# DeltaNet and a cosine router with experts: the last tile of each expert joined with the one before it, at widths sorted by size

## The chip, the cores and the metric

The kernel runs on one core of a Trainium2 chip. It is judged by the device time of one execution, in microseconds; several executions are taken and their median is given. TensorE (PE) multiplies matrices, VectorE (DVE) and ScalarE (ACT) work on rows of up to 128 partitions, GpSimd (POOL) issues the indirect transfers here, and SyncE (SP) issues the direct ones.

## The reference

Two blocks follow each other. The first is a delta-rule attention over 4 batches, 8 heads, 768 steps and 48 dimensions a head:

```python
k_n = k / (norm(k) + 1e-6)
for t in range(S):
    y[t] = q[t] @ state
    v_old = state.T @ k_n[t]
    state += beta[t] * outer(k_n[t], v[t] - v_old)
```

Its output, 3072 tokens of 384 numbers, goes through a router that sends each token to one of 8 experts (384 to 1024 to 384), all in float32:

```python
logits = normalized(x) @ normalized(expert_emb).T / tau
expert_idx = argmax(logits)
gate_w = softmax(logits)[expert_idx]
for e in range(8):
    mask = expert_idx == e
    out[mask] = gate_w[mask] * (relu(x[mask] @ w1[e]) @ w2[e])
```

On the given inputs the reference sends 385, 377, 351, 388, 365, 351, 421 and 434 tokens to experts 0 to 7.

## The kernel before, in words

**Attention and routing.** The 768 steps are cut into chunks of 64, and 24 units (12 chunks times two pairs of sequences, 128 tokens each) are worked through. A planner (`Plan`) holds every operation of this part with a cost and a due time and writes out one order for each engine. After each group of four units (two at the end) the router runs: TensorE counts for each token its place among those of its expert, and POOL writes the token's row number into a list in DRAM (`idmap`, one list of 3200 places for each expert, filled up with entries that point to an empty row and to no output). `run` holds where each list has got to. Token rows with their gate stand in DRAM too (`x_dram`).

When 16 of the 24 units are routed, `snap` notes how many tokens of expert 0 there are, at most 256 (`ahead`), and two early tiles of 128 of them are computed within the attention part, out of weights kept in `w1_first` and `w2_first`.

**Expert stage.** The rest begins when the last tokens are on the lists (line 1101 on). Here the order on each engine is the order of the code. The tiles are of 128 tokens of one expert. DVE works out on one partition how many tiles each expert has (`tiles`, at least one), a running sum over experts (`ends`, lines 1189 to 1191, seven additions one after another), and from it for every tile number the expert and the place of its list (`info`). SP reads these into registers (`where`, lines 1126 and 1127) and issues the read of the tile's list (`read_ids`); POOL gathers its rows by that list (`read_x`); SP loads the expert's two matrices, 1.5 MB each, into rings of three (`read_w1`, `read_w2`).

A tile then has three steps on TensorE: `transposed` turns its rows (three transposes, a copy by DVE), `hidden` makes 24 matmuls of 128 columns into two PSUM banks (a ReLU by ACT each), and `result` makes eight matmuls of 384 columns into one bank; DVE multiplies by the gate and POOL scatters the rows to the output. In `work_through` the order is: gather for tile i+3, hidden of i, first matrix of i+3, transposes of i+1, result of i, second matrix of i+3, list of i+5. The first tile takes its weights from `w1_first` and `w2_first`.

There are up to 31 tiles. The first 22 always run; four more run if there are more than 22 (line 1256), five more if there are more than 26 (line 1258). The branches read the number from a register that every engine has loaded (line 1227).

## Time and profile before

| | |
|---|---|
| median of 9 runs | 645.83 us (641.39 to 649.39) |
| profiled execution | 641.89 us, span 640.2 us |
| granted TensorE clock, mean over the span | 0.912 |
| TensorE busy | 546.0 us (85%) |
| DVE, ACT, POOL busy | 42%, 28%, 26% |
| expert stage | first transposes at 340.4 us, last result at 626.8 us, end 640.2 us |
| tiles in the expert stage | 26 |
| moved by DMA | 115.46 MB, of which 50 loads of 1.5 MB are experts' matrices |

The times of an operation are from one profiled execution. A record of TensorE is one pass; a float32 matmul shows as two records. Records overlap, so the distance from one start to the next tells what a record costs, and not its own length. "Idle before" is the time in which an engine stood still ahead of an operation, with what ended it.

### The profile page before, as it was taken

What the parts mean: (1) busy time and instruction counts of PE and PEld (TensorE: products, weight loads), DVE (VectorE), ACT (ScalarE), POOL (GpSimd) and SP (SyncE); (2) the same over time, 40 slices, a digit from 0 to 9 for tenths busy, and PEclk for the clock granted to TensorE, in tenths of its full rate; (3) what the DMA queues carried; (4) which work ended last, traced back from release to release, by engine and by line L of the source; (5) the groups of instructions that cost most, each with busy time, mean ns of one, the idle gap of its engine ahead of it and who ended that gap; (6) DMA issues with size and microseconds to landing.
All of it is one profiled execution on the core that took longest, in us unless ns stands there. A gap on an engine that the chain in (4) does not pass through costs nothing. (4 is left out here: it accounts for less than half of the span.)

```text
span 640.2 us, 22729 instructions
## 1 busy us (share of the span) xinstructions
PE 546.0 (85%) x9995; PEld 459.4 (72%) x9995; DVE 267.2 (42%) x749; ACT 180.1 (28%) x327; POOL 167.7 (26%) x217
## 2 busy tenths in 40 slices
PE   3573688688788888788997999999999999999991
PEld 3462678587677877677875787878787878787880
DVE  4898768669889877823141111010111111111100
ACT  2222535526637345464420010101111111111010
POOL 4434334154362221312121211212121212121100
PEclk9995788559989779989997999999999999999996
DMA  4444744533414311132015999999999899999500
GB/s 75 81 80 85 198 73 78 128 63 67 107 36 103 93 45 26 64 98 81 31 40 199 390 387 388 387 348 304 339 319 333 305 341 319 337 312 331 201 17 6
DMA packets 127911, 115.46 MB, mean 180 GB/s; under 512 B 83754, under 2 KB 113873, under 8 KB 127810
## 3 DMA queue, kind: packets, MB, share of 16 engines
q1 hardware_dynamic: 122242, 102.93, 52.0%
q0 software_dynamic: 4480, 10.85, 4.6%
q8 instruction: 80, 1.31, 0.8%
q10 hardware_dynamic: 1088, 0.20, 0.2%
q14 instruction: 21, 0.17, 0.1%
HBM read 102.02 MB, written 12.72 MB: 179 GB/s over the span
## 5 line engine op out<-in xcount | busy, mean ns | idle before, releaser
L1164 ACT ACTIVATE hT<-acc 128x512 f32<-128x512 f32 x52 | 31.1, 597 | 259.5 <-PE acc L1162 259.5
L1162 PEld LDWEIGHTS acc<-xTm,w 128*128 128x128 f32 x816 | 93.8, 192 | 4.5
L1162 PE MATMUL acc<-xTm,w 128*128 128x128 f32 x816 | 93.9, 275 | 0.0
L1169 PE MATMUL acc<-w,hT 128*128 128x384 f32 x272 | 90.5, 486 | 0.0
L1172 POOL DMA_INDIRECT out_dram<-y,ids x26 | 26.3, 1010 | 205.2 <-DVE y L1171 195.4
L1169 PEld LDWEIGHTS acc<-w,hT 128*128 128x128 f32 x272 | 50.4, 190 | 31.5
L1154 DVE COPY xTm<-acc 128x384 f32<-128x384 f32 x26 | 14.5, 558 | 134.6 <-PE acc L1153 134.6
L565 DVE TENSOR_TENSOR w_first<-w_first,tmp 128x30 f32<-128x30 f32 (+9 forms) x180 | 68.3, 381 | 3.9
L561 DVE TENSOR_TENSOR tmp<-w_first 128x30 f32<-128x30 f32 (+9 forms) x180 | 67.2, 375 | 4.1
L1171 DVE TENSOR_SCALAR y<-acc,xg 128x384 f32<-128x384 f32 x26 | 16.1, 618 | 125.0 <-PE acc L1169 125.0
L273 PE MATMUL psum_pair<-KQ 48*32 48x64 f32 (+2 forms) x2304 | 50.2, 280 | 15.2 <-DVE w_first L546 7.2
L273 PEld LDWEIGHTS psum_pair<-KQ 48*32 48x32 f32 (+1 forms) x2304 | 42.9, 142 | 20.6 <-issue 9.5
L1162 PEld LDWEIGHTS acc<-xTm,w_first 128*128 128x128 f32 x432 | 51.5, 198 | 3.3 <-DVE xTm L1154 1.2
L1162 PE MATMUL acc<-xTm,w_first 128*128 128x128 f32 x432 | 51.7, 281 | 0.8 <-DVE xTm L1154 0.8
L1169 PE MATMUL acc<-w_first,hT 128*128 128x384 f32 x144 | 47.9, 486 | 0.0
L273 PE MATMUL psum_pair<-S,KQ 48*64 48x64 f32 x1408 | 34.7, 243 | 9.4 <-issue 4.1
L1169 PEld LDWEIGHTS acc<-w_first,hT 128*128 128x128 f32 x144 | 26.7, 190 | 16.7
L273 PEld LDWEIGHTS psum_pair<-S,KQ 48*64 48x64 f32 x1408 | 29.8, 154 | 12.2 <-issue 5.3
L276 ACT ACTIVATE KQ<-psum_pair 128x1024 f32<-128x1024 f32 x24 | 24.6, 1024 | 44.8 <-PE psum_pair L309 35.3
L1137 POOL DMA_INDIRECT xg<-x_dram,ids x26 | 25.3, 972 | 38.5 <-DMA ids<-idmap 22.9
L960 POOL DMA_INDIRECT idmap<-tokid,slots_i x24 | 24.1, 1006 | 39.1 <-DVE slots_i L936 12.6
L615 POOL TENSOR_TENSOR V<-v,sqb 128x384 f32<-128x384 f32 x24 | 20.6, 864 | 50.3 <-DVE R L670 32.6
(183 smaller groups left out, 737.4 us busy)
## 6 DMA issues: line engine op xcount, KB each, us to landing
w<-in_moe_w_dram SPq DMA_DIRECT2D x34, 1536.0 KB
w_first<-in_moe_w_dram SPq DMA_DIRECT2D x16, 1536.0 KB
q<-in_q_dram SPq DMA_DIRECT2D x96, 48.0 KB
v<-in_v_dram SPq DMA_DIRECT2D x48, 96.0 KB
w_first<-in_k_dram SPq DMA_DIRECT2D x88, 48.0 KB
x_dram<-XC SPq DMA_DIRECT2D x5, 800.0 KB
idmap<-space SPq DMA_DIRECT2D x1, 2048.0 KB
w_first<-in_moe_w_dram SPq DMA_DIRECT2D x6, 256.0 KB
```

The source lines that it names most:

```text
L273: nc.tensor.matmul(out_, lhsT=lhsT, rhs=rhs, start=start, stop=True, skip_group_check=True)
L276: nc.scalar.activation(out_, in_, ACT.Copy, scale=scale)
L561: nc.vector.tensor_tensor(t, X[:, j + 1:, j:j + 1].broadcast_to([128, rows, j]), X[:, j:j + 1, 0:j].broadcast_to([128, rows, j]), op=ALU.mult)
L565: nc.vector.tensor_tensor(X[:, j + 1:, 0:j], X[:, j + 1:, 0:j], t, op=ALU.subtract)
L615: nc.gpsimd.tensor_tensor(buf("V", m)[:, i * 2 * NP * D:(i + 1) * 2 * NP * D].rearrange("p (jj j d) -> p jj j d", jj=2, d=D), buf("v", m)[ ...
L960: put = nc.gpsimd.indirect_dma_start(out=idmap[:, :], out_offset=bass.IndirectOffsetOnAxis(ap=slot_i[:, i:i + 1], axis=0), in_=K["tokid"][ ...
L1137: t.read = nc.gpsimd.indirect_dma_start(out=t.x, out_offset=None, in_=x_dram[:, :], in_offset=bass.IndirectOffsetOnAxis(ap=t.ids[:, 0:1], ...
L1162: nc.tensor.matmul(psH[:, i, :], lhsT=t.w1[:, j, (f + i) * 128:(f + i + 1) * 128], rhs=t.xT[:, j, :], start=(j == 0), stop=(j == KC - 1))
L1164: nc.scalar.activation(t.hT[:, f:f + 4, :], psH, ACT.Relu)
L1169: nc.tensor.matmul(psO, lhsT=t.hT[:, f, :], rhs=t.w2[:, f, :], start=(f == 0), stop=(f == NF - 1))
L1171: nc.vector.tensor_scalar_mul(y, psO, t.x[:, Dm:Dm + 1])
L1172: nc.gpsimd.indirect_dma_start(out=out[:, :], out_offset=bass.IndirectOffsetOnAxis(ap=t.ids[:, 1:2], axis=0), in_=y, in_offset=None, bound ...
```

## The change

The two early tiles stay. After them:

- The tile that follows takes 160 tokens of expert 0 (`FIRST`). What is left of each expert's list is cut into whole tiles of 128 and one tail that is whatever remains after them, between 129 and 256 tokens for the larger experts, less for a short list, and zero or below where nothing is left. So the number of whole tiles is the number of 128s less two, at least zero.
- Tails are ranked by size on DVE and run from the largest to the smallest at fixed widths, 256, 256, 224, 224, 192, 192, 160 and none (`WIDTHS`). Where a tail doesn't fit its width (`misfit`), another arm of a branch runs eight tails of 256.
- In a tile of more than 128 tokens the hidden layer is made in matmuls as wide as the tile, two of them to a PSUM bank. The rows are gathered, transposed and scattered in blocks of up to 128.
- The result of a block of 128 is as before. One of 96, 64 or 32 rows is made in parts of 64 and 32: with 64 rows, matmuls go by turns to the two column halves of the array (PSUM partitions 0 to 63 and 64 to 127), with 32 to its four quarters, and the partial sums are added by ACT and DVE.
- The order: the first tile, five whole tiles, the tails, then the whole tiles that remain, in a branch for more than five and one for more than ten. Rings are made a class, so that both arms of the branch begin at the same buffer; the index buffers for items from the fourth on are 16 new ones, gathered rows have 10 buffers in place of 6, results 6 in place of 4.
- The running sum is one multiplication with a triangle of ones (`not_after`) and one reduction. 16 operations on DVE are added that work out and sort the tails, ten on POOL and one on DVE that set constants, and one in `snap`. Two numbers are loaded into registers on every engine in place of one.
- Item 3's rows are gathered twice: once ahead of `chain` and once by it, into the same buffer.

The core of the diff:

```diff
+FIRST = 160
+WIDTHS = (256, 256, 224, 224, 192, 192, 160, 0)
...
-    nth = cpool.tile([1, NT, 1], F32, name="nth")
+    nth = cpool.tile([1, WHOLE, 1], F32, name="nth")
...
         nc.gpsimd.memset(zrow, 0.0)
+        nc.gpsimd.memset(not_after, 1.0)
+        nc.gpsimd.affine_select(out=not_after, in_=not_after, compare_op=ALU.is_ge, fill=0.0, base=0,
+                                pattern=[[1, E], [-1, E]], channel_multiplier=0)
+        for i, w in enumerate(WIDTHS):
+            nc.gpsimd.memset(widths[:, i:i + 1], float(w))
 
...
     def snap():
         nc.vector.tensor_scalar_min(ahead, run[0:1, 0:1], float(AHEAD * T))
         nc.vector.tensor_copy(ahead_i, ahead)
+        nc.vector.tensor_scalar_add(base_e[:, 0:1], ahead, float(FIRST))
 
...
-    w1_ring = ring("w1_", 3, [128, KC, F], ex, first=[w1_first])
-    w2_ring = ring("w2_", 3, [128, NF, Dm], ex, first=[w2_first])
-    x_ring = ring("xg", 6, [128, ROW], ex)
-    xT_ring, hT_ring, y_ring = (ring(name, n, shape, ex) for name, n, shape in (
-        ("xTm", 2, [128, KC, T]), ("hT", 2, [128, NF, T]), ("y", 4, [128, Dm])))
-    banks = ring("acc", 8, [128, 512], pe)
+    class Ring:
+
+        def __init__(r, name, n, shape, pool, dtype=F32, first=()):
+            r.ts = list(first) + [pool.tile(shape, dtype, name=f"{name}{i}") for i in range(n - len(first))]
+            r.taken = 0
+            turning.append(r)
+
+        def __call__(r):
+            r.taken += 1
+            return r.ts[(r.taken - 1) % len(r.ts)]
+
+    turning = []
+    w1_ring = Ring("w1_", 3, [128, KC, F], ex, first=[w1_first])
+    w2_ring = Ring("w2_", 3, [128, NF, Dm], ex, first=[w2_first])
+    x_ring = Ring("xg", 10, [128, ROW], ex)
+    more_ids = Ring("more_ids", 16, [128, ID], ex, I32)
+    xT_ring, hT_ring, y_ring, part_ring = (Ring(name, n, shape, ex) for name, n, shape in (
+        ("xTm", 2, [128, KC, 2 * T]), ("hT", 2, [128, NF, 2 * T]), ("y", 6, [128, Dm]), ("part", 6, [128, Dm])))
+    banks = Ring("acc", 8, [128, 512], pe)
 
...
     class Tile:
-        pass
-
-    def where(t, i):
-
-        if i == 0:
+
+        def __init__(t, width, place):
+            t.width, t.place, t.ids, t.x = width, place, [], []
+
+    def sizes(t):
+        return [min(T, t.width - o) for o in range(0, t.width, T)]
+
+    def where(t):
+        kind, i = t.place
+        if kind == "first":
             t.e, t.s = 0, nc.values_load(ahead_i[0:1, 0:1], engines=(SP,), min_val=0, max_val=AHEAD * T)
         else:
-            t.e = nc.values_load(info[0:1, 0, i:i + 1], engines=(SP,), min_val=0, max_val=E - 1)
-            t.s = nc.values_load(info[0:1, 1, i:i + 1], engines=(SP,), min_val=0, max_val=NMAP - T)
-
-    def read_ids(t):
-        t.ids = ids_ring()
-        read = nc.sync.dma_start(t.ids, idmap[bass.ds(t.s, T), :])
-        for put in lists[-1]:
-            tc.add_manual_dep(read.ins, put.name, AFTER, reason="tokens' lists are complete")
+            table = info if kind == "whole" else ends_info
+            t.e = nc.values_load(table[0:1, 0, i:i + 1], engines=(SP,), min_val=0, max_val=E - 1)
+            t.s = nc.values_load(table[0:1, 1, i:i + 1], engines=(SP,), min_val=0, max_val=NMAP - 2 * T)
+
+    def read_ids(t, source):
+        where(t)
+        for b in range(len(sizes(t))):
+            t.ids.append(source())
+            read = nc.sync.dma_start(t.ids[b], idmap[bass.ds(t.s + b * T, T), :])
+            for put in lists[-1]:
+                tc.add_manual_dep(read.ins, put.name, AFTER, reason="tokens' lists are complete")
 
     def read_x(t):
-        t.x = x_ring()
-        t.read = nc.gpsimd.indirect_dma_start(
-            out=t.x, out_offset=None, in_=x_dram[:, :],
-            in_offset=bass.IndirectOffsetOnAxis(ap=t.ids[:, 0:1], axis=0))
+        for b in range(len(sizes(t))):
+            t.x.append(x_ring())
+            t.read = nc.gpsimd.indirect_dma_start(
+                out=t.x[b], out_offset=None, in_=x_dram[:, :],
+                in_offset=bass.IndirectOffsetOnAxis(ap=t.ids[b][:, 0:1], axis=0))
 
...
     def transposed(t):
         t.xT = xT_ring()
-        psX = acc([128, KC, 128])
-        for j in range(KC):
-            nc.tensor.transpose(psX[:, j, :], t.x[:, j * 128:(j + 1) * 128], ident)
-        nc.vector.tensor_copy(t.xT, psX)
+        for b, n in enumerate(sizes(t)):
+            psX = acc([128, KC, 128])
+            for j in range(KC):
+                nc.tensor.transpose(psX[:, j, 0:n], t.x[b][0:n, j * 128:(j + 1) * 128], ident[0:n, 0:n])
+            nc.vector.tensor_copy(t.xT[:, :, b * T:b * T + n], psX[:, :, 0:n])
 
     def hidden(t):
         t.hT = hT_ring()
-        for f in range(0, NF, 4):
-            psH = acc([128, 4, T])
-            for i in range(4):
+        k = 4 if t.width <= T else 2
+        for f in range(0, NF, k):
+            psH = acc([128, k, t.width])
+            for i in range(k):
                 for j in range(KC):
-                    nc.tensor.matmul(psH[:, i, :], lhsT=t.w1[:, j, (f + i) * 128:(f + i + 1) * 128], rhs=t.xT[:, j, :],
-                                     start=(j == 0), stop=(j == KC - 1))
-            nc.scalar.activation(t.hT[:, f:f + 4, :], psH, ACT.Relu)
+                    nc.tensor.matmul(psH[:, i, :], lhsT=t.w1[:, j, (f + i) * 128:(f + i + 1) * 128],
+                                     rhs=t.xT[:, j, 0:t.width], start=(j == 0), stop=(j == KC - 1))
+            nc.scalar.activation(t.hT[:, f:f + k, 0:t.width], psH, ACT.Relu)
+
+    def columns(n):
+        if n in (T, T // 2, T // 4):
+            return [(0, n)]
+        return [(0, T // 2), (T // 2, T // 4)]
 
     def result(t):
-        psO = acc([128, Dm])
-        for f in range(NF):
-            nc.tensor.matmul(psO, lhsT=t.hT[:, f, :], rhs=t.w2[:, f, :], start=(f == 0), stop=(f == NF - 1))
-        y = y_ring()
-        nc.vector.tensor_scalar_mul(y, psO, t.x[:, Dm:Dm + 1])
-        nc.gpsimd.indirect_dma_start(
-            out=out[:, :], out_offset=bass.IndirectOffsetOnAxis(ap=t.ids[:, 1:2], axis=0),
-            in_=y, in_offset=None, bounds_check=N - 1, oob_is_err=False)
-
+        for b, n in enumerate(sizes(t)):
+            y = y_ring()
+            for o, w in columns(n):
+                q = T // w
+                psO = acc([128, Dm])
+                for f in range(NF):
+                    c = f % q * w
+                    nc.tensor.matmul(psO[c:c + w, :], lhsT=t.hT[:, f, b * T + o:b * T + o + w], rhs=t.w2[:, f, :],
+                                     start=(f < q), stop=(f >= NF - q))
+                if q == 1:
+                    nc.vector.tensor_scalar_mul(y, psO, t.x[b][:, Dm:Dm + 1])
+                    continue
+                total = psO[o:o + w, :]
+                for i in range(q):
+                    if i * w != o:
+                        part = part_ring()[o:o + w, :]
+                        nc.scalar.copy(part, psO[i * w:i * w + w, :])
+                        nc.vector.tensor_tensor(y[o:o + w, :], total, part, op=ALU.add)
+                        total = y[o:o + w, :]
+                nc.vector.tensor_scalar_mul(total, total, t.x[b][o:o + w, Dm:Dm + 1])
+            nc.gpsimd.indirect_dma_start(
+                out=out[:, :], out_offset=bass.IndirectOffsetOnAxis(ap=t.ids[b][0:n, 1:2], axis=0),
+                in_=y[0:n, :], in_offset=None, bounds_check=N - 1, oob_is_err=False)
+
+    first = Tile(FIRST, ("first", 0))
+    read_ids(first, ids_ring)
+    first.w1, first.w2 = w1_ring(), w2_ring()
+    read_x(first)
 
     nc.vector.tensor_tensor(run, run, base_e, op=ALU.subtract)
-    nc.vector.tensor_tensor(run[:, 0:1], run[:, 0:1], ahead, op=ALU.subtract)
+    over = thr.rearrange("p e n -> p (e n)")
     nc.vector.tensor_tensor(thr, run.unsqueeze(2).broadcast_to([1, E, N // T]), thr, op=ALU.is_gt)
     tiles = cpool.tile([1, 1, E], F32, name="tiles")
     nc.vector.tensor_reduce(tiles[:, 0, :], thr, axis=AX.X, op=ALU.add)
-    nc.vector.tensor_scalar_max(tiles[:, :, 0], tiles[:, :, 0], 1.0)
+    nc.vector.tensor_scalar(tiles, tiles, -2.0, 0.0, op0=ALU.add, op1=ALU.max)
     ends = cpool.tile([1, 1, E], F32, name="ends")
-    nc.vector.tensor_copy(ends, tiles)
-    for e in range(1, E):
-        nc.vector.tensor_tensor(ends[:, :, e], ends[:, :, e], ends[:, :, e - 1], op=ALU.add)
-    te = [1, NT, E]
-    done = cpool.tile(te, F32, name="done")
-    nc.vector.tensor_tensor(done, ends.broadcast_to(te), nth.broadcast_to(te), op=ALU.is_le)
-    which = cpool.tile([1, NT], F32, name="which")
+    upto = over[:, 0:E * E].rearrange("p (a b) -> p a b", a=E)
+    nc.vector.tensor_tensor(upto, tiles.broadcast_to([1, E, E]), not_after, op=ALU.mult)
+    nc.vector.tensor_reduce(ends[:, 0, :], upto, axis=AX.X, op=ALU.add)
...
+    whole = [Tile(T, ("whole", i)) for i in range(WHOLE)]
+    read_ids(whole[0], ids_ring)
+    read_x(whole[0])
+    tc.add_manual_dep(read_w1(whole[0]).ins, whole[0].read.ins.name, AFTER, reason="first tokens, then weights")
+    read_w2(whole[0])
+    read_ids(whole[1], ids_ring)
+    read_x(whole[1])
+    read_w1(whole[1])
+    read_w2(whole[1])
+
+    vals = cpool.tile([1, 3, E], F32, name="vals")
+    nc.vector.tensor_copy(vals[:, 0], sixteenths)
+    nc.vector.scalar_tensor_tensor(out=vals[:, 1], in0=tiles[:, 0], scalar=float(T), in1=base_e, op0=ALU.mult, op1=ALU.add)
+    nc.vector.scalar_tensor_tensor(out=vals[:, 2], in0=tiles[:, 0], scalar=-float(T), in1=run, op0=ALU.mult, op1=ALU.add)
+    nc.vector.tensor_tensor(vals[:, 2], vals[:, 2], sixteenths, op=ALU.subtract)
+    nc.vector.tensor_tensor(upto, vals[:, 2:3].broadcast_to([1, E, E]),
+                            vals[:, 2].unsqueeze(2).broadcast_to([1, E, E]), op=ALU.is_gt)
...
+    ends_info = cpool.tile([1, 2, E], I32, name="ends_info")
+    nc.vector.tensor_copy(ends_info, sorted_[:, 0:2])
+    misfit = cpool.tile([1, 2], F32, name="misfit")
+    nc.vector.tensor_tensor(sorted_[:, 2], sorted_[:, 2], widths, op=ALU.is_gt)
+    nc.vector.tensor_reduce(misfit[:, 0:1], sorted_[:, 2], axis=AX.X, op=ALU.add)
+    nc.vector.tensor_copy(misfit[:, 1:2], ends[:, 0, E - 1:E])
+    flags = cpool.tile([1, 2], I32, name="flags")
+    nc.vector.tensor_copy(flags, misfit)
+
+    transposed(first)
+
+    def chain(items, start, stop):
+
+        for i in range(start, stop):
+            t = items[i]
+            if i + 3 < len(items):
+                read_x(items[i + 3])
+            hidden(t)
+            if i + 3 < len(items):
+                read_w1(items[i + 3])
+            if i + 1 < len(items):
+                transposed(items[i + 1])
+            result(t)
+            if i + 3 < len(items):
+                read_w2(items[i + 3])
+            if i + 5 < len(items):
+                read_ids(items[i + 5], more_ids)
+
+    ahead_of_tails = 5
+    tails = [Tile(2 * T, ("end", i)) for i in range(E)]
+    items = [first] + whole[:ahead_of_tails] + tails
+    for t in items[3:5]:
+        read_ids(t, more_ids)
+    read_x(items[3])
+    bad, count = (nc.values_load(flags[0:1, i:i + 1], min_val=0, max_val=most) for i, most in ((0, E), (1, WHOLE)))
+    chain(items, 0, 1 + ahead_of_tails)
+
+    def arm(ws):
+
+        was = [r.taken for r in turning]
+        own = [copy.copy(t) for t in items[1 + ahead_of_tails:]][:len(ws)]
+        rest = [copy.copy(t) for t in whole[ahead_of_tails:]]
+        for t in own + rest:
+            t.ids, t.x = list(t.ids), list(t.x)
+        for t, w in zip(own, ws):
+            t.width = w
+        line = own + rest[:ahead_of_tails]
+        chain(line, 0, len(own))
+        with tc.If(count > ahead_of_tails):
+            chain(line, len(own), len(line))
+            with tc.If(count > 2 * ahead_of_tails):
+                line = rest[ahead_of_tails:]
+                for t in line[:5]:
+                    read_ids(t, more_ids)
+                for t in line[:3]:
+                    read_x(t)
+                    read_w1(t)
+                    read_w2(t)
+                transposed(line[0])
+                chain(line, 0, len(line))
+        for r, n in zip(turning, was):
+            r.taken = n
+
+    with tc.If(bad == 0) as cmp:
+        arm([w for w in WIDTHS if w])
+    with cmp.Else():
+        arm([2 * T] * E)
```

## The prediction

> **What bounds the kernel now.** I read the page's slices first (the TensorE row stands at 9 from 300 us on), then the busy time by stretch, then what TensorE waited for, then its timeline. The stretch from the first full-clock tile to the last matmul:
>
> ```profile
> 366.00:627.00 261.00, 260.75 (x1608) 209.26 (x1606) 27.89 (x48) 28.67 (x48) 44.69 (x45) 1.00 0.88 308
> ```
>
> The columns are PE, weight load, DVE, ACT, POOL, granted clock, DMA share, GB/s. TensorE is busy for all but 0.25 us of 261 at a granted clock of 1.00; DVE, ACT and POOL stand at a tenth to a sixth. DMA is loaded (0.88), but it does not hold TensorE up. From 340 us to 627 us TensorE's waits are these:
>
> ```profile
> PE acc L1153 <- DMA xg<-x_dram,ids: 4.4, 2, 3.9
> PE acc L1162 <- DVE xTm L1154: 0.8, 1, 0.8
> ```
>
> 3.9 and 0.8 of that belong to the start; no wait for weights (the DMA of `w`) is among them. So in this stage time is columns streamed through TensorE, and one tile is read off its start times:
>
> ```profile
> 366.57 5.52 PE L1162 MATMUL acc<-xTm,w 128*128 128x128 f32 x48
> 371.93 0.49 PE L1153 MATMUL acc<-ident,xg 128*128 128x128 f32 x3
> 372.26 5.33 PE L1169 MATMUL acc<-w,hT 128*128 128x384 f32 x16
> 377.42 5.52 PE L1162 MATMUL acc<-xTm,w_first 128*128 128x128 f32 x48
> ```
>
> Start to start: hidden 5.36 (48 records, two to a float32 matmul: 111.7 ns each at 128 columns), transposes 0.33 (0.11 each), result 5.16 (16 records, 322.5 ns each at 384 columns). A tile is 10.85 us, and 26 of them are 282.1. The two durations give a line for other widths: 6.3 ns + 0.823 ns a column.
>
> **What the inputs make of the code.** The reference's choices on the given inputs count 385, 377, 351, 388, 365, 351, 421 and 434 tokens for the eight experts. Less the 256 of expert 0 done early, that is 2+3+3+4+3+3+4+4 = 26 tiles, as the trace has (26 of L1172). After: a first tile of 160; 10 whole tiles; tails of 249, 237, 223, 223, 178, 165, 132 (expert 0 has none left), which fit widths 256, 256, 224, 224, 192, 192, 160 and drop the eighth. Columns fall from 3328 to 2944, weight pairs loaded from 25 to 17; row blocks gathered and scattered stay 26.
>
> **TensorE's work after.** By the line, a record at 160, 192, 224, 256 columns is 138.1, 164.4, 190.7, 217.1 ns; 48 of them 6.63, 7.89, 9.16, 10.42. A full block's result is 5.16. A remainder of 64 columns puts two matmuls on two column halves, one of 32 puts four on quarters; at full overlap that is 2.58 and 1.29. Transposes are 0.33 a block, less for narrow ones. So:
> 256: 10.42 + 10.32 + 0.66 = 21.40, twice 42.80.
> 224: 9.16 + 5.16 + 2.58 + 1.29 + 0.59 = 18.78, twice 37.56.
> 192: 7.89 + 5.16 + 2.58 + 0.51 = 16.14, twice 32.28.
> 160: 6.63 + 5.16 + 1.29 + 0.43 = 13.51, and the first tile the same.
> With 10 × 10.85 = 108.5 the sum is 248.2, which is **33.9 less** than 282.1.
>
> **The packing** is the price that the trace of before does not show: it never runs 128 rows on column groups. The nearest rows are the attention's, with rows and columns both split:
>
> ```profile
> 205.25 1.16 PE L273 MATMUL psum_pair<-S,KQ 48*64 48x64 f32 x64
> ...
> 175.25 2.15 PE L273 MATMUL psum_pair<-KQ 48*32 48x64 f32 x128
> ```
>
> The first: 64 records on four tiles in 1.16 us, about 15 ns each once the last one's 0.2 us latency is taken off, where one alone streams about 56 ns (half of 111.7): 3.7 of 4. The second has four column groups times two row halves, at half clock (a record alone is 112 ns): 16.8 ns each, over six of eight. So four column groups stream different data at once, but each over 48 rows. Ends: full overlap, no gain beyond it (the array has no more columns); or none, where all eight remainders cost 5.16, which is 4 × 2.58 + 4 × 3.87 = 25.8 more. I take 3.7 of 4, nearest to the first row: 7% of 15.5, or **+1.0**.
> The Trainium skill, "TensorE: Matmul & The Clock Gate", Part 3, "Measured speedup vs the span model", speaks against this: three column tiles of 32 gave 2.38, not 3. Taken for all remainders, my estimate from that page is +4.0 in place of +1.0, and the forecast would be 620.
>
> **Changing between array shapes.** Start to start, 128*128 transposes to 64*64 costs 0.20 us against 0.11 streaming, so 0.09 more; 48*64 of 96 columns (streaming 0.08) to 128*128 costs 0.25, so 0.17 more. The remainders make 14 changes (3 for each 224, 2 for each other); transposes of 64 and 32 rows up to 12 more. Ends 14 × 0.09 = 1.3 and 26 × 0.17 = 4.4; I take 20 × 0.13, **+2.6**.
>
> **Evictions.** A tail's hidden layer fills four banks of two slices; the ReLU of the last is needed by result matmul 6, some 3.9 us after the first, and an ACTIVATE takes 0.6. The partial sums add up to 4 ACT copies and 7 DVE operations a tile (0.56 to 0.62 for 384 columns), 2 and 4 us beside a step of 13 to 21 us on engines that are at 11%. Queued behind them is the next ReLU or xTm copy, whose reader comes 5 us later. 0; if that cover went, 4 us a tail.
>
> **The start.**
>
> ```profile
> 336.95 0.99 POOL L1137 DMA_INDIRECT xg<-x_dram,ids  x1 [4.88 <-PE psum_pair L1045]
> 338.25 1.01 POOL L1053 DMA_INDIRECT out_dram<-space,ids  x1 [0.31 <-issue]
> 339.56 0.99 POOL L1137 DMA_INDIRECT xg<-x_dram,ids  x1 [0.30 <-issue]
> 340.42 0.50 PEld L1153 LDWEIGHTS acc<-ident,xg 128*128 128x128 f32 x3 [4.48 <-issue]
> ```
>
> The first tile's second block is gathered in the slot of 338.25 (the early tile's store moves behind), lands 3.45 later as the first one did, at 341.7, is transposed and copied, and each engine now loads two flags (0.49 each on TensorE). Hidden starts at about 343.1 in place of 342.13: +1.0 (ends 0.2 and 1.9). POOL's queue gets a trap: item 3's tokens are gathered twice into the same buffer. The index rows of that tile are now issued behind two pairs of weights on SP's queue; one pair held an index row up from 346.1 to 354.8 before, so they land near 362, the first gather near 368 and the second near 374.4 (6.4 us to landing each), while TensorE wants them at 343.1 + 15.5 (tile one, at half clock to 346.2) + 10.85 + 5.36, about 374.8. Behind the second gather on POOL stand the stores of the first tile (nobody waits) and the next gather, wanted 11 us later. 0 to 3, taken 0.5. The old 0.7 wait at 361 goes. Sum **+0.8**.
>
> **What lies beside other work.** DVE's index chain ran from 329.02 to 335.17. Seven serial adds and wider compares go (some 2.4 us), two go in; then 16 operations for the tails, 0.13 to 0.41 each, 2.1 to 6.6. It ends between 336 and 340.5, before the flags are loaded at about 341.8; SP's first index load follows its own issue at 334.95 as before. The early tile's multiply, queued behind, is up to 4 us late and only its store waits. 0. Ten constants on POOL (0.09 to 0.42 each) fall before an idle time of 7.8 us at 20.7; one on DVE (0.15) before one of 1.0. 0. The add in the snapshot is 0.2 at most. SP issues 16 DMAs of weights fewer. Branches that fall through cost TensorE 0.09 (the one at 579.0), and the taken one cost 3.37 us but beside other work:
>
> ```profile
> L1258 PEldq COMPARE_BRANCH x2: 193/1781/3369, 622.3 to 626.9; - x2
> ```
>
> After the last matmul come another branch or two on POOL before the end (0.05 each as POOL's were, 3.4 as the PE's): **+0.5**.
>
> **Sum.** 33.9 - 1.0 - 2.6 - 0.8 - 0.5 = 29.0 less. The profiled execution took 641.9 us (span 640.2), so 612.9 on its scale. The median of the nine runs is 645.8, 3.9 above it; the attention part is left alone, so I subtract the same 29.0: **616.8**, say 617.
>
> **Rivals.**
> *Column groups overlap in part.* If four quarters run only two at a time (each float32 matmul is two records on one quarter, which may block the order), four remainders cost 2.58 in place of 1.29: +5.2, 622; half the overlap everywhere gives 630. For it: no row has 128-row column tiles. Against: 3.7 of 4 also with two records a matmul.
> *They don't overlap.* +25.8 less the 1.0 booked: 642, 0.6% faster.
> *Slower: the tails do not fit.* If the chip's counts put a sorted tail above its width (223 against 224 is the closest, twice), the other arm runs eight tails of 256: 171.2 + 108.5 + 13.5 = 293.2, 11.1 more than before; with 3.4 for the taken branch, 0.8 and 0.5 it is 662. It decides from two tokens routed differently from the reference. Against: tokens on the edge between two experts are few, and the trace's 26 tiles agree with the counts.
> *A new wait for tokens.* The doubled gather lands 5 us late: 622. For it: DMA share 1.04 from 355 to 367 us. Against: 17 weight pairs for 25, and tail steps of 13 to 21 us each need no more than one pair.
>
> **How the numbers follow.** Near-full overlap 0.68; partial overlap 0.15; none 0.07; wrong arm 0.05; new waits 0.05. The likeliest gives 617, by its own bounds 611 to 622. Partial overlap and new waits reach to 632; with them 0.88 is counted, the ends of each cut off, so 609 to 632 for 8 in 10. A measurement of this kernel tells about 0.5%, 3.2 us, from no change. Faster: all but the wrong arm and half of no overlap, 0.91; same 0.04; slower 0.05.
>
> **What would show it.** TensorE busy without a gap at clock 1.00 from 366 us to about 598; 256-wide hidden records near 217 ns; a 32-column remainder in 1.3 to 1.5 us and not 2.6 or 5.2; gaps of 0.1 to 0.2 where the shape changes; DMA share near 0.6; whole tiles still 10.85. It is wrong if remainders take over 3 us, if seven tails turn into eight of 256, or if TensorE waits for `xg` near 375.

## The result, and the profile after

The changed kernel takes 619.19 us (median of 20 runs, 615.21 to 623.23) where the kernel before took 646.36 beside it (62 runs). The ratio is 0.960, with a 95% interval of 0.958 to 0.962: 25.9 us less, 24.7 to 27.2. The forecast was 29.0 less. The profiled execution of the changed kernel took 617.59 us with a span of 615.7; that of the kernel before had 640.2.

The busy time by stretch, changed kernel, for the stretch that answers to 366 to 627 us before, and for the start of the experts' tiles (columns as there: PE, weight load, DVE, ACT, POOL, granted clock, DMA share, GB/s):

```profile
366.00:600.00 234.00, 234.00 (x1279) 179.24 (x1278) 33.02 (x63) 32.89 (x61) 47.08 (x48) 1.00 0.69 241
...
340.00:355.00 15.00, 9.61 (x45) 9.13 (x46) 1.34 (x3) 1.05 (x3) 3.94 (x4) 0.66 0.65 225
```

TensorE is still the bound: busy for all of 234 us at clock 1.00, with 1279 records where the longer stretch before had 1608. DVE and ACT have risen only from 27.9 and 28.7 to 33.0 and 32.9 us, so the added copies and sums are far from a limit, and the DMA share fell from 0.88 to 0.69. The second row is the one place in the expert stage, up to its last matmul, where the clock is down; it is taken up below.

What TensorE waited for from 338 us to the end:

```profile
PE acc L1190 <- DMA xg<-x_dram,ids: 4.9, 2, 4.2
PE acc L1200 <- DVE xTm L1191: 0.6, 1, 0.6
```

Both rows belong to the first tile (4.2 and 0.7 for its two blocks of tokens, 0.6 for the copy). The 0.7 that the kernel before waited for tokens at 361 us is gone. Nothing waits near 375, where the prediction had put the danger of the doubled gather; the transposes that need those tokens came later, at 379.57, and the second gather was issued at 373.45.

TensorE's timeline through one tail of each width:

```profile
439.30 10.52 PE L1200 MATMUL acc<-xTm,w 128*128 128x256 f32 x48
449.66 0.74 PE L1190 MATMUL acc<-ident,xg 128*128 128x128 f32 x6
450.24 10.51 PE L1217 MATMUL acc<-w,hT 128*128 128x384 f32 x32
460.58 9.24 PE L1200 MATMUL acc<-xTm,w 128*128 128x224 f32 x48
469.66 0.74 PE L1190 MATMUL acc<-ident,xg 128*128 128x128 f32 x6
470.24 9.51 PE L1217 MATMUL acc<-w,hT 128*128 128x384 f32 x48
479.68 9.35 PE L1200 MATMUL acc<-xTm,w_first 128*128 128x224 f32 x48
...
507.78 8.16 PE L1217 MATMUL acc<-w,hT 128*128 128x384 f32 x32
515.87 8.07 PE L1200 MATMUL acc<-xTm,w 128*128 128x192 f32 x48
523.77 0.79 PE L1190 MATMUL acc<-ident,xg 128*128 128x128 f32 x6
524.49 8.16 PE L1217 MATMUL acc<-w,hT 128*128 128x384 f32 x32
532.58 6.79 PE L1200 MATMUL acc<-xTm,w_first 128*128 128x160 f32 x48
539.21 0.49 PE L1190 MATMUL acc<-ident,xg 128*128 128x128 f32 x3
539.53 6.75 PE L1217 MATMUL acc<-w_first,hT 128*128 128x384 f32 x32
546.22 5.62 PE L1200 MATMUL acc<-xTm,w 128*128 128x128 f32 x48
```

Read start to start, as in the prediction. The hidden layers take 10.36, 9.08, 7.90 and 6.63 us (10.42, 9.16, 7.89 and 6.63 by the line), so the line through two widths holds out to 256 columns, within 0.08 us. The result of a 160-column tail takes 539.53 to 546.22, 6.69: one full block of 5.16 and 1.53 for the 32-row remainder. That of a 192-column tail takes 8.09: 5.16 and 2.93. That of a 224-column tail takes 9.44: 5.16 and 4.28. These rows carry one form's name (128x384), and the names of the narrower forms do not show; the count does, x48 for three parts and x32 for two.

The start of the first tile (brackets: what ended the idle time before):

```profile
334.55 5.33 PE L1059 MATMUL psum_pair<-w_first,space 128*128 128x384 f32 x16
344.08 0.87 PE L1190 MATMUL acc<-ident,xg 128*128 128x128 f32 x3 [4.21 <-DMA xg<-x_dram,ids]
345.64 0.53 PE L1190 MATMUL acc<-ident,xg 32*128 32x32 f32 x3 [0.69 <-DMA xg<-x_dram,ids]
346.79 9.62 PE L1200 MATMUL acc<-xTm,w_first 128*128 128x160 f32 x48 [0.62 <-DVE xTm L1191]
356.25 0.49 PE L1190 MATMUL acc<-ident,xg 128*128 128x128 f32 x3
356.58 6.75 PE L1217 MATMUL acc<-w_first,hT 128*128 128x384 f32 x32
363.26 5.62 PE L1200 MATMUL acc<-xTm,w 128*128 128x128 f32 x48
...
595.07 5.33 PE L1217 MATMUL acc<-w,hT 128*128 128x384 f32 x16
```

The first row is the early tile's result and the last row the last tile's. The first tile has the second gather, transposes and copy that the prediction priced, and a hidden layer of 9.46 us (to 356.25), where 160 columns at full clock take 6.63.

For all that follows I cut each trace at three marks: the end of the early tile's result (the last row of 16 result records ahead of the expert stage, which ends at 336.56 us before and 339.88 after), the start of the second tile, and the end of the last result matmul (5.16 us behind its row's start). In us, of single profiled executions:

| kernel | ratio to before (95%) | early result's end to span's end | second tile to last matmul | last matmul to span's end |
|---|---|---|---|---|
| before | 1 | 303.64 | 271.58 | 13.62 |
| changed | 0.960 (0.958 to 0.962) | 275.82 | 236.97 | 15.47 |
| changed, again (another chip) | 0.956 (0.951 to 0.961) | 275.59 | 236.94 | 15.31 |
| remainders unpacked | 0.981 (0.975 to 0.987) | 290.20 | 247.54 | 15.71 |
| all tails 256 | 0.994 (0.991 to 0.997) | 296.28 | 257.61 | 15.40 |
| other arm | 1.023 (1.018 to 1.028) | 318.12 | 280.91 | 14.25 |
| no conditions | 0.951 (0.947 to 0.955) | 270.58 | 237.71 | 9.98 |
| long filler | 0.957 (0.954 to 0.961) | 276.49 | 237.16 | 15.35 |
| one gather, full rows | 0.955 (0.950 to 0.959) | 274.03 | 236.48 | 15.33 |
| all three edits | 0.960 (0.955 to 0.964) | 275.42 | 236.49 | 15.11 |
| the same, short filler | 0.950 (0.944 to 0.956) | 272.39 | 236.48 | 14.82 |
| before with the constants | 1.002 (0.998 to 1.005) | 303.89 | 270.92 | 13.64 |

Ratios are of fast executions alone: one that took over 1.5% longer than the fastest of its kernel is left out.

From the early result on, 27.8 us are saved in this pair of executions. The attention part ahead of it ended 3.3 us later in the changed kernel's execution (339.88 against 336.56), which is why the two spans differ by 24.5 only. The chips differ: the kernel before took 646, 661, 662 and 648 us beside these runs, so ratios and stages are compared, not times. Where a time is given for an experiment below, it is its ratio times 646.36.

### The profile page after: what moved, and what is told of

The parts are those of the page before. It is cut to its first block, busy times and chain, and to the rows that moved or that the text cites. A ratio compares the mean times of both kernels' runs of the same rounds, so it can differ in the third digit from the quotient of the medians.

```text
span 615.7 us, 21947 instructions
## 1 busy us (share of the span) xinstructions
PE 512.9 (83%) x9643; PEld 422.5 (69%) x9643; DVE 275.8 (45%) x778; ACT 185.1 (30%) x343; POOL 168.5 (27%) x228
## 5 line engine op out<-in xcount | busy, mean ns | idle before, releaser
L1200 PEld LDWEIGHTS acc<-xTm,w 128*128 128x128 f32 x576 | 77.7, 191 | 5.8 <-issue 1.8
L1202 ACT ACTIVATE hT<-acc 128x512 f32<-128x512 f32 (+3 forms) x52 | 28.5, 548 | 174.9 <-PE acc L1200 174.8
L1200 PE MATMUL acc<-xTm,w 128*128 128x128 f32 (+3 forms) x576 | 80.3, 299 | 0.0
L1217 PE MATMUL acc<-w,hT 128*128 128x384 f32 (+2 forms) x272 | 78.9, 489 | 0.0
L1230 POOL DMA_INDIRECT out_dram<-y,more_ids x22 | 21.7, 986 | 160.8 <-DVE y L1220 127.8
L1217 PEld LDWEIGHTS acc<-w,hT 128*128 128x128 f32 (+2 forms) x272 | 42.2, 176 | 30.3 <-issue 5.8
L1200 PE MATMUL acc<-xTm,w_first 128*128 128x128 f32 (+3 forms) x288 | 47.3, 327 | 0.6 <-DVE xTm L1191 0.6
L1217 PE MATMUL acc<-w_first,hT 128*128 128x384 f32 (+2 forms) x176 | 44.2, 489 | 0.0
L283 ACT ACTIVATE KQ<-psum_pair 128x1024 f32<-128x1024 f32 x24 | 24.5, 1023 | 44.4 <-PE psum_pair L316 36.4
L1217 PEld LDWEIGHTS acc<-w_first,hT 128*128 128x128 f32 (+2 forms) x176 | 23.1, 163 | 17.8 <-issue 4.5
L469 POOL TENSOR_TENSOR rt<-rn,half 128x32 f32<-128x32 f32 x4 | 22.0, 5488 | 30.6 <-DVE rn L454 30.6
```

What stands on the lines that cost most here:

```text
L283: nc.scalar.activation(out_, in_, ACT.Copy, scale=scale)
L469: nc.gpsimd.tensor_tensor(out=flat(rt, part), in0=flat(ss, part), in1=half[:, 0:w], op=ALU.pow)
L1200: nc.tensor.matmul(psH[:, i, :], lhsT=t.w1[:, j, (f + i) * 128:(f + i + 1) * 128], rhs=t.xT[:, j, 0:t.width], start=(j == 0), stop=(j == K ...
L1202: nc.scalar.activation(t.hT[:, f:f + k, 0:t.width], psH, ACT.Relu)
L1217: nc.tensor.matmul(psO[c:c + w, :], lhsT=t.hT[:, f, b * T + o:b * T + o + w], rhs=t.w2[:, f, :], start=(f < q), stop=(f >= NF - q))
L1230: nc.gpsimd.indirect_dma_start(out=out[:, :], out_offset=bass.IndirectOffsetOnAxis(ap=t.ids[b][0:n, 1:2], axis=0), in_=y[0:n, :], in_offse ...
```

## The experiments

**Remainders unpacked.** Does the packing into column halves and quarters work, or would joining alone give the gain?

```
-            for o, w in columns(n):
-                q = T // w
+            for o, w in [(0, n)]:
+                q = 1
...
-                    nc.vector.tensor_scalar_mul(y, psO, t.x[b][:, Dm:Dm + 1])
+                    nc.vector.tensor_scalar_mul(y[0:n], psO[0:n], t.x[b][0:n, Dm:Dm + 1])
```

> The changed kernel, but each remainder of 96, 64 or 32 rows is made by one matmul for each hidden slice, of as many columns as the remainder has, on one column group; no partial sums are added. Theory (column groups overlap in full, two of two and four of four): the remainders go from 3.87, 2.58 and 1.29 us to 5.16 us each, two of 96, two of 64 and two of 32 rows, +15.5; some fewer changes of shape, about -1: 619 becomes 633 to 634, and a remainder takes 5.2 us in the timeline. Rival (groups take turns and the gain comes from joining alone): no change, 619. Half the overlap: +7, 626.

Measured: ratio 0.981, which is 634 us, and from the early result on 14.4 us more than the changed kernel. The 160-column tail in its timeline:

```profile
554.59 6.79 PE L1200 MATMUL acc<-xTm,w_first 128*128 128x160 f32 x48
...
561.54 10.60 PE L1217 MATMUL acc<-w_first,hT 128*128 128x384 f32 x32
572.07 5.62 PE L1200 MATMUL acc<-xTm,w 128*128 128x128 f32 x48
```

Its result takes 10.53 us in place of 6.69: the 32-row remainder costs as much as a full block, 3.84 us more than in quarters. A 192-column tail costs 19.20 in place of 16.74. For 224 columns the gain of the packing is smaller, 20.00 against 19.10 and 20.26 against 19.45: the remainder of 96 goes in two parts, halves and quarters, and pays one change of shape more. The rivals of no overlap and of half overlap both fall.

**All tails 256 wide.** What is the finer width worth, beside the joining?

```
-WIDTHS = (256, 256, 224, 224, 192, 192, 160, 0)
+WIDTHS = (256, 256, 256, 256, 256, 256, 256, 0)
```

> The changed kernel with all seven tails 256 columns wide: joined with the tile before, but not sorted into finer widths; column groups are left to the first tile alone. Theory (time is columns streamed): seven tails of 21.3 us, 149 in place of 128.3, +21: 619 becomes 640, so that joining alone is worth only about 6 of the 27 us. Rival (what pays is fewer tiles and fewer weight loads, 17 pairs for 25): it stays within 5 us of 619.

Measured: ratio 0.994, 642 us, and 20.5 more than the changed kernel from the early result on. Every tail takes the same time; two starts show it:

```profile
477.53 10.52 PE L1200 MATMUL acc<-xTm,w 128*128 128x256 f32 x48
...
498.87 10.52 PE L1200 MATMUL acc<-xTm,w_first 128*128 128x256 f32 x48
```

21.34 us, almost exactly two old tiles (21.70). Joining saves a third of a microsecond a pair, 2.5 us for seven. More comes from expert 0: by the reference's count it has 129 tokens left behind the early tiles, so the kernel before ran a whole tile of 10.85 us for one token, where the first tile's 32 further columns cost 2.66 by the prediction's line (13.51 less 10.85). 17 pairs of weights in place of 25 shorten nothing here, in a stage in which TensorE never waited for weights. With the run before, the gain divides so: of 27.8 us from the early result on, 7.4 come with joining at 256 and the first tile of 160, and 20.5 with the finer widths and their packing. 6.1 of these are left (296.28 against 290.20) when all packing is taken away, the first tile's too.

**The other arm.** The prediction's slower rival, with its price.

```
-            nc.gpsimd.memset(widths[:, i:i + 1], float(w))
+            nc.gpsimd.memset(widths[:, i:i + 1], 0.0)
```

> The changed kernel with all widths that the flag is compared with set to 0, so that the given inputs go through the other arm: eight tails of 256, the eighth empty of tokens. Theory of the prediction's slower rival: 8 x 21.3 = 170.7 in place of 128.3, +42.4, with the taken branch at the entry to the arm bare on TensorE (3.4 to 4.3 us): 662 to 665. Rival (the branch is hidden or the empty tile costs less): 640 to 658.

Measured: ratio 1.023 (1.018 to 1.028), 661 us: slower than before, as priced, had the tails not fitted. The eight tails cost what was said: from the early result on it is 42.3 us more than the changed kernel, where 42.4 was said for them. The taken branch did not: it is in the first row, and what TensorE waited behind it in the second. The third row is the branches at the end of the arm, which this kernel falls through last.

```profile
L1359 PEldq COMPARE_BRANCH  x1: 6267/6267/6267, 430.2 to 430.2; - x1
```

```profile
PE acc L1200 <- DMA w<-in_moe_w_dram: 1.4, 1, 1.4
```

```profile
L1346 PEldq COMPARE_BRANCH  x2: 193/1919/3645, 656.7 to 661.3; - x2
```

TensorE's sequencer took the branch at 430.2, some 5 us before the matmuls already queued had run out, and needed 6.3 us to be at the other arm. Only 1.4 us of that was bare. (The wait is put down to the weights' DMA; the tile ahead of it took 12.72 us for 11.17.) So this taken branch in the middle cost much less than its duration; what conditions cost at the end, the next run shows.

**No conditions.** Where do the 1.9 us at the end come from?

```
-        with tc.If(count > ahead_of_tails):
-            chain(line, len(own), len(line))
...
+        chain(line, len(own), len(line))
...
-    with tc.If(bad == 0) as cmp:
-        arm([w for w in WIDTHS if w])
-    with cmp.Else():
-        arm([2 * T] * E)
+    arm([w for w in WIDTHS if w])
```

> The changed kernel with the arm of sorted widths alone and no conditions around the tiles behind the tails; it leaves out the code for other counts of tokens. After the last matmul the changed kernel takes 15.5 us to the end and the one before 13.6; after its last scatter POOL stands 3.5 us before its next instruction. Theory A (the taken branches over code that is not run cost that, on POOL and TensorE): the end shrinks to 12 us or less, and the time to 615 to 616. Theory B (the end waits for the last scatter to land, whatever the branches): 15 us and 619 remain. Either way the gap of 0.1 us ahead of the tile behind the last tail goes.

Measured: ratio 0.951, 615 us; the end takes 9.98 us in place of 15.47. The sequencers' instructions behind the last tile, for the changed kernel (the end of its conditions, then of the program), and the last of this kernel (columns: count, shortest, median and longest in ns, first and last start):

```profile
L1346 POOLq EVENT_SEMAPHORE  x4: 17/43/43, 604.8 to 605.0; - x4
L1346 PEldq COMPARE_BRANCH  x2: 3771/4032/4293, 596.0 to 600.6; - x2
L1346 DVEq COMPARE_BRANCH  x2: 47/57/67, 600.4 to 601.5; - x2
L1346 POOLq INC_SWDGE_SEM  x1: 1870/1870/1870, 605.4 to 605.4; - x1
```

```profile
L1388 POOLq DRAIN  x3: 46/103/7079, 607.8 to 615.4; - x3
```

```profile
L1374 POOLq DRAIN  x3: 46/109/8235, 618.5 to 627.3; - x3
```

In the changed kernel the order on POOL's queue is: last scatter at 601.33, its first semaphore wait at 604.8, the semaphore increment from 605.4 to 607.3, and only then a drain of 7.08 us, which ends the program. In the kernel before the long wait began at 627.7, straight behind the scatter, ended at 630.1, and the drain began at 632.4. Without conditions the drain begins at 618.5, ahead of the last scatter, and runs beside it. So the end shrinks as theory A said, and by more: the conditions cost 5.5 us there. Its reason, taken branches, covers only a part. The waits and the increment that close a condition stand ahead of the drain in the kernel before too, which with 13.62 paid 3.6 of the 5.5. The change's own share is 1.85. TensorE takes 4.29 us for its last branch (its longest before was 3.37), but it is through at 604.9, while POOL drains from 607.8. What grew is on POOL's queue: from the scatter's start to the increment it took 4.1 us (601.33 to 605.4), before 2.7 (627.68 to 630.4). The other arm's kernel, which has the same conditions but jumps over no arm last, ends in 14.25, so 1.2 of the 1.85 go with the arm that lies behind. In that kernel POOL's first wait begins 0.2 us behind the scatter's start (662.27 and 662.05), in the changed kernel 3.5 behind it. That the jump over the arm is what holds POOL up there is the likeliest reading, but POOL's own branches take 38 and 50 ns, and no run separates it.

The expectation of the gap of 0.1 us ahead of the tile behind the last tail was wrong: that tile takes 10.95 with the conditions and without. It is a change of shape, from quarters to the full array. This run also shows a wait that the changed kernel's did not, here with the two gathers ahead of it:

```profile
PE acc L1190 <- DMA xg<-x_dram,more_ids: 0.6, 1, 0.6
```

```profile
384.23 0.95 POOL L1173 DMA_INDIRECT xg<-x_dram,more_ids  x1 [7.78 <-DMA more_ids<-idmap]
390.55 0.95 POOL L1173 DMA_INDIRECT xg<-x_dram,more_ids  x1 [5.36 <-DMA xg<-x_dram,more_ids]
```

It is at the fourth tile's tokens, those gathered twice: the second gather waits until the first has landed, and TensorE's transposes begin at 396.94, 6.4 us behind it.

**Filler, gather, transposes.** Three runs on the start.

```
     plan.emit(warm)
+    unused = psum[[i for i in range(4) if i != plan.held[("early_o", 1)]][0]]
+    for _ in range(18):
+        mm(unused[:, 0, 0:256], ident, half_wide)
...
             nc.vector.tensor_copy(t.xT[:, :, b * T:b * T + n], psX[:, :, 0:n])
+            if t is first:
+                for _ in range(2):
+                    mm(banks.ts[7][:, 0:256], ident, half_wide)
```

> The changed kernel with 22 matmuls of 256 columns whose result nobody reads, in TensorE's idle time between the early tile's result and the first tile: 18 behind the result, 2 behind each of the first tile's two blocks of transposes. Theory (the first hidden layer takes 9.46 us for 6.63 because the granted clock falls to half in the 5.6 us ahead of it): the clock stays at 1.00, the first hidden takes 6.6 to 7, 2.5 to 2.8 us less. Rival (the clock falls by an older history, or the filler delays the transposes): the first tile's result begins no earlier after the early result's end than in the changed kernel, 16.4 us, and the time is the same.

Measured: the clock stayed up and the first hidden layer took 6.52 us; and the filler took too long. A float32 matmul is two records, so 18 of 256 columns ran 7.87 us, and the transposes began 7.87 us behind the early result in place of 4.2. From the early result's end to the first tile's first result matmul it took 17.3 us, against 16.7 in the changed kernel. The theory on the clock and the rival on the delay are both right, and cancel: ratio 0.957.

```
-                nc.tensor.transpose(psX[:, j, 0:n], t.x[b][0:n, j * 128:(j + 1) * 128], ident[0:n, 0:n])
+                nc.tensor.transpose(psX[:, j, :], t.x[b][:, j * 128:(j + 1) * 128], ident)
...
-    read_x(items[3])
```

> The changed kernel without the second gather of the fourth tile's tokens, and with the transposes of narrow blocks made on all 128 rows. Theory: the gather costs nothing (no wait for tokens near 375 us in the trace of the changed kernel), 0; the transposes of a tail of 224, 192 or 160 take 0.50 to 0.52 us in place of 0.58 to 0.75, so 0.5 to 1.0 us for the seven. Rival (the doubled gather delays the stores and gathers behind it, in a way that the waits of TensorE don't show): 2 us or more.

Measured: from the second tile to the last matmul 236.48 in place of 236.97, 0.49 less, in the tails of 192 (16.54 for 16.74 and 16.71) and one of 224 (19.26 for 19.45): the low end of what was expected. The doubled gather seems to cost something at times: the tile during which the fourth tile's tokens are transposed took 10.84 to 10.88 us in four of seven executions that gather twice, and 11.07, 11.19 and 11.62 in the others; in the three that gather once, 10.85 each time. That is 0 to 0.8 us, 0.2 in the mean. In the two longest the profile puts a wait of TensorE down to those tokens (0.6 and 0.1 us); with so few executions the size is rough.

> The changed kernel with the edits of the two runs before together: filler matmuls ahead of the first tile, one gather of the fourth tile's tokens, transposes on all rows. It does all of the reference's work for all counts of tokens. If both theories hold, 3 to 4 us less than the changed kernel; if the filler does not keep the clock, less than 1.

Measured: the tails gain as in the run before, the start loses as in the one with the filler: 275.42 from the early result on, ratio 0.960.

**Short filler**, beside the changed kernel on the same chip. The edit is against the run with all three edits:

```
-    for _ in range(18):
+    for _ in range(9):
...
-                for _ in range(2):
+                for _ in range(1):
```

> As the run with all edits together, but 9 filler matmuls behind the early result in place of 18 and 1 in place of 2 behind each block of transposes: a float32 matmul of 256 columns is two records, 0.43 us and not 0.22, so that 18 ran 7.8 us past an idle time of 4.2. Theory: 9 take 3.9 us and end before the tokens land; from the early result's end (the filler left out) to the first tile's first result matmul it takes 13.2 to 13.6 us, where the changed kernel and five kernels made from it took 15.5 to 16.7; with the 0.5 us of the tails, 2.5 to 3.5 us less than the changed kernel. Rival (the clock still falls in what is left of the idle time): 15.5 or more, and no gain but 0.5.

> The changed kernel itself, on the same chip as the run with the short filler: the ratio to the kernel before that it had elsewhere, 0.960 within 0.4%, for both theories.

Measured, the timeline of the short filler, then of the changed kernel on the same chip:

```profile
345.74 4.05 PE L280 MATMUL psum_pair<-half,ident 128*128 128x256 f32 x18
350.50 0.52 PE L1193 MATMUL acc<-ident,xg 128*128 128x128 f32 x3 [0.71 <-DMA xg<-x_dram,ids]
...
353.39 6.76 PE L1206 MATMUL acc<-xTm,w_first 128*128 128x160 f32 x48
```

```profile
345.08 0.88 PE L1190 MATMUL acc<-ident,xg 128*128 128x128 f32 x3 [4.08 <-DMA xg<-x_dram,ids]
...
347.91 9.59 PE L1200 MATMUL acc<-xTm,w_first 128*128 128x160 f32 x48 [0.71 <-DVE xTm L1191]
```

The busy time by stretch over the 20 us from the early result on, the short filler first (the figure behind POOL's is the granted clock):

```profile
346.00:366.00 20.00, 18.33 (x103) 14.21 (x105) 2.26 (x5) 1.75 (x4) 4.91 (x5) 1.00 0.74 256
```

```profile
341.00:361.00 20.00, 14.49 (x69) 12.69 (x69) 1.99 (x4) 1.75 (x4) 4.91 (x5) 0.74 0.78 270
```

The clock stands at 1.00 in place of 0.74, the first hidden layer takes 6.60 in place of 9.43, and the first result begins 14.40 us behind the early result in place of 16.66. That is more than the 13.2 to 13.6 expected, because the tokens came 0.5 us later in this execution, 1.0 of waiting for the second block is left, and the copy follows it. From the early result on it is 3.2 us less (272.39 against 275.59), within the 2.5 to 3.5 expected. The times do not settle it: the ratios, 0.950 (0.944 to 0.956) and 0.956 (0.951 to 0.961), overlap, and over all six runs each the medians are 619.05 and 618.75. The changed kernel's 0.956 lies at the edge of the 0.4% around 0.960 that was said. The attention part, the same instructions in both, ended at 345.91 in the one and at 341.01 in the other profiled execution. The gain is shown in the stage; in the whole it is below what six runs can tell.

**Before with the constants.** Do the added constants move the attention part?

```
+        nc.gpsimd.memset(not_after, 1.0)
+        nc.gpsimd.affine_select(out=not_after, in_=not_after, compare_op=ALU.is_ge, fill=0.0, base=0,
...
+            nc.gpsimd.memset(widths[:, i:i + 1], float(32 * i))
+        nc.vector.tensor_scalar_mul(sixteenths, iota_e[0:1], 1.0 / 16.0)
+        nc.vector.tensor_scalar_add(after_first, ahead, 160.0)
```

> The kernel before with the constants that the change adds: the ten fills and the mask on POOL, the sixteenths on DVE and one addition at the snapshot; nothing reads them. In the two profiled executions the attention part ended 3.3 us later in the changed kernel. Theory (that is one execution against another; the constants fall in idle time): ratio 1.000, within 0.3%. Rival (they push the schedule's start): up to 3.3 us, 1.005.

Measured: ratio 1.002 (0.998 to 1.005), between 1.2 us less and 3.4 more. The interval holds the theory, and does not quite shut out the rival.

## Why the prediction was right

The time lies within the range and inside the likeliest case's own bounds (611 to 622); the saving was put 3.1 us too high against the first measurement, 0.4 against the second (28.6, with an interval of 25.5 to 31.8). By its steps, each against the two profiled executions:

- *TensorE's work, 33.9 less.* Right: the hidden layers came within 0.08 us of the line, a tail of 256 took 21.34 and 21.28 us in all (21.40 said), whole tiles 10.85. All tails fitted, and the count of tiles was as worked out from the reference.
- *Packing, +1.0.* Wrong, it is 0: two of two and four of four run together. In the trace's records two 64-column matmuls start 6.5 ns apart and the next two 323 ns later; four 32-column ones start within 20 ns of each other, and the next four 323 ns later. 323 ns is what one full matmul of 384 columns takes alone (322.5). The 3.7 of 4 came from a row of small matmuls, 56 ns long; with records of 323 ns nothing of that loss is seen. The Trainium skill's figure ("TensorE: Matmul & The Clock Gate", Part 3, "Measured speedup vs the span model": 2.38 for three column tiles) made it +4.0 by the prediction's estimate. Here the measurement decides, and four quarters give 4. That the total by that estimate, 620, lies nearer to the measured 619 than the forecast of 617 does is chance.
- *Changes of shape, +2.6.* Nearly right. From the second tile to the last matmul, 236.97 is 2.65 more than the lengths by the line (234.32: the sum less the first tile and the second's transposes), and the first tile adds 0.12 (13.53 with the clock up, 13.41 by the line): 2.8 in all, for the 3.6 that packing and shapes were given together. The results take 0.24 more than the streaming for the two changes of a 160-column tail, 0.35 for the two of a 192 and 0.41 or 0.49 for the three of a 224, so 0.12 to 0.17 a change, where 0.13 was taken. The narrow transposes were priced by their rows. That held for 96 rows (0.58, at 469.66, for 0.59) and failed for fewer: a full and a 64-row block took 0.74 and 0.75 us where 0.51 was said, a full and a 32-row block 0.72 (523.77 to 524.49) where 0.43 was said, more than two full ones (0.66).
- *The start, +0.8.* The hidden layer began 1.34 us later behind the early result (+1.0 said), the old wait of 0.7 is gone as said, and the doubled gather cost 0.03 (0.5 said, 0 to 0.8 in other executions). Unpriced was the clock: the first hidden layer lost 2.9 us to it, the kernel before 2.0. The loss was 2.0 to 2.9 us in the nine executions without filler, 2.0 and 2.8 of them in the kernel before and the one with the constants, so no cost of the change is seen in it.
- *The end, +0.5.* The worst step. It measured +1.85. Only TensorE's branch was seen to be long, and taken to be beside other work; POOL's queue was priced at 0.05 a branch, from a kernel in which no arm lay behind it. The row that would have told is the one behind the branch: POOL waits, increments a semaphore and drains, one after another.
- *Evictions, index chain, constants, weights.* 0 each. For evictions and weights the waits bear it out: TensorE waits for neither ACT nor DVE nor weights behind the first tile. For the constants the run with them leaves up to 3.4 us open, and no run took the index chain alone.

Sum of what was measured: 33.9 - 2.8 - 1.6 (1.34 + 0.03 + 0.92 for the clock - 0.7) - 1.85 = 27.7, against the 27.8 between the marks. The total came so near partly by luck: packing and shapes were 0.8 us too dear and the start 0.8 too cheap, which cancel, and the end's 1.35 is what is left. What is left to the 25.9 of the runs lies in the attention part, by subtraction; it was 3.3 us later in the profiled pair. Four kernels that share its instructions ended it anywhere from 351.6 to 357.1 us on one chip, so differences of that size come from execution to execution; on another chip three more ended it at 352.0 to 353.6, and the kernel before with the constants at 351.1. Whether a part of 1 to 2 us belongs to the change is not settled.

The rivals: no overlap (642) and overlap in part (622 to 630) fell with the unpacked remainders at 634; the slower one (662) has the price it was given (661), though its branch left 1.4 us bare in place of 3.4, but the tails fit; the new wait for tokens (622) is seen in two executions, at up to 0.8 us, not 5.

## What to carry to other kernels

Where TensorE is busy at full clock without a wait, a tile's time follows from a price a column read off the start times of two widths, and here a change of tile widths was priced to about one per cent from that (234.32 us for 236.97). Packing remainders of 32 or 64 rows on column groups then gave what it promised, less 0.12 to 0.17 us for each change of shape. Price the end of the program as carefully as the stage: what came behind the last matmul ran one instruction after another on POOL's queue, and conditions around the last tile lengthened it. And look at the granted clock in the first rows behind an idle time, since 4 us of idling cost another 2.0 to 2.9 here.

## What the runs showed of the hardware

- Column groups with 128 rows run fully together at 384 columns: two matmuls of 64 columns or four of 32 in 323 ns.
- Behind the last matmul the programs with conditions took 13.6 to 15.7 us to the end, and the one without 10.0, since POOL's drain of 8.2 us then starts ahead of the last scatter.
- A taken branch took TensorE's sequencer 6.3 us in the middle, of which 1.4 were bare, because the matmuls already queued ran on meanwhile.
- In the changed kernel the granted clock fell to half at 342.4 us, 2.5 us into 4.2 us without matmuls, and stayed there for 10.2 us; in six of the nine executions without filler it stayed for 6.8. Nine float32 matmuls in the first gap and one in each of the two gaps behind it kept it at 1.00.
- In three of seven executions the step that needs the tokens gathered twice took 0.2 to 0.8 us longer; the three executions with one gather show none of it.
